# A spectral transformer block: another queue for an early load, full-height line products, new planner ranks, and another order in two feed-forward items

## The chip, the cores and the metric

The kernel runs on one NeuronCore of a Trainium2 chip. Five engines work side by side, each with its own queue that is worked off in order: TensorE (PE, matrix products, with weight loads listed as PEld), VectorE (DVE), ScalarE (ACT), GpSimd (POOL) and SyncE (SP, which here only starts transfers). SP, ACT and POOL can all start DMA transfers. The engines wait for each other by semaphores. The metric is the device time of one execution in microseconds (us); the profile gives one such execution, with every instruction's start and length.

## What is computed

The input is x with 2048 rows of 512 values (S = 2048, D = 512), the inner width of the feed-forward is F = 1792. Everything is 32-bit floating point. Cut to what matters, the reference is:

```python
mod = (silu(c) @ w_mod).reshape(1, 6, 1, -1)
sa, ca, ga, sb, cb, gb = (mod[:, n] for n in range(6))

h = layernorm(x) * (1 + ca) + sa
a = einsum("bsd,ed->bse", h, dft_hid_re)
b = einsum("bsd,ed->bse", h, dft_hid_im)
y = einsum("ts,bse->bte", dft_seq_re, a) - einsum("ts,bse->bte", dft_seq_im, b)
x = x + ga * y

h = layernorm(x) * (1 + cb) + sb
gate, up = h @ w1, h @ w3
x = x + gb * ((silu(gate) * up) @ w2)
```

So there is a Fourier mixing step along both axes (a product with the 512x512 and then with the 2048x2048 DFT matrices, of which only the real part is kept), and then a gated feed-forward, each behind a layer norm that is scaled and shifted by six vectors computed from c.

## The kernel before

**Precision.** Each 32-bit operand is split into a rounded high part (made by ACT) and the remaining low part (made by DVE or POOL as a subtraction). A product is then three passes on PE: high by high, low by high, high by low (`PASSES`). So each operand costs an ACT and a DVE or POOL instruction before PE can use it.

**Symmetry.** The kernel uses the symmetries of the DFT matrices: rows and mirrored rows of x are summed and subtracted, and a part of the sequence DFT is handled apart as "lines". Because it relies on these symmetries it checks the given matrices while it runs (instructions at line 1708, the tiles cx, cy, cz, cv). `judge` (lines 1759 to 1795) turns the outcome into one flag, by a chain of some twenty small DVE instructions. A branch at the end, taken only if the flag is set, holds a general version.

**The planned stage.** The first part, up to the first eleven products of the feed-forward, is a list of about 900 steps (`task`), each with a rank, the steps that it needs, and the engines that can do it, with a cost for each. Many can be done by DVE or POOL. `arrange` (lines 187 to 276) turns the list into an order when the program is built. It looks at all steps whose needs are met, takes those that could begin within 0.3 us of the soonest, and among them the one with the lowest rank, then the earliest end. The sum of a base rank, `KIND_BY[kind]` and `STEP_BY[name]` is the rank. The planner's own clock starts from times written by hand (`at(...)`, `clear.update(...)`). [...] To the end of a POOL candidate it adds `LOCK`. The order that comes out is fixed: on the chip each engine does its instructions in that order and waits where it must. Where the plan shows PE idle in the first part, the program puts filler products in (`keep_warm`, line 599).

Ahead of the planned steps stand some written in a fixed order (lines 447 to 459 and 2204 to 2229): the first loads, twelve filler products of 128x512, the statistics, root and scaling of row block 0, its transposes on PE (`turn_rows`, line 827), and the vectors sa and ca (scaled rows of w_mod summed by `mod_add`, line 626, and by PE, `mod_sum`, line 637). `load_x(1)` starts on SP only the loads of one side of row block 1. Those of the other side are started by ACT (`load_side(1, nc.scalar)`, line 2211), behind the statistics of block 0 and ahead of its square root (`norm_root`, line 792). The hidden DFT's blocks (`load_hid`, line 394) follow on SP. They are read by `shift_product` (line 729) and scaled by `w_highs` and `w_lows`.

The hidden DFT of block k is `hid_product` (line 929) and `hid_difference` (line 948). The sequence DFT comes in eight pieces (b, o): `seq_piece` (line 1295) and then `seq_lines` (line 1325), which adds the lines. In `seq_lines` the products with `sel` have 64 rows (the contraction runs over 64 partitions), their neighbours 128. `sel` holds one nonzero per column, made by `count_columns` and `spread_lines`. It multiplies `yc`, the first 64 partitions of a tile `gm_tile`, whose other half holds nothing.

Behind the sequence DFT stands the second layer norm for row blocks b = 0 and 1: `all_gates` and `add_rows` (DVE, line 1431), squares and root on ACT, scaling, transposes (`turn_block`, line 1474), the modulated tiles `xc`, their split (`h2h`, `h2l`), the sums of `xc` (tasks `tt`) and the split of these (`th`, `tl`). The copies `xm` (`keep_sums`) save x for the output. The tasks `jw1` and `jw3` split the first weights w1 and w3, with their sums `w1s` and `w3s` (`weight_jobs`).

**The feed-forward.** It has 14 items (g, pair): for each pair of row blocks, seven slices g of 256 of the 1792 inner columns. For gate (`a`) and up (`b`) an item has seven products instead of eight, a scheme with sums of operands: `a1` to `a7` and `b1` to `b7`, each two times three passes of 512 columns, 1.36 us of PE. `TO` names the bank into which a product accumulates: 1, 6, 7 and 4 into one, 2 into a second, 5 and 3 into a third. A result of the second row block is the first bank behind 1, 6 and 7 plus product 5. Before the change, 5 is copied out by ACT and added by DVE to the bank when 7 is there:

```python
dst = vs[i][q][:, k, :] if w == "w1" else own
plus(dst, to, own)          # DVE reads the bank `to`
result(i, w, q, k, dst)
```

The `b` results are multiplied with the gate's and split into `hf`, by `behind(1, ...)` on ACT and `behind(2, ...)` on DVE, one and two units later in the program. A `y` is one product with w2 (`down_unit`, six passes), and for the last two slices of the second pair DVE adds its result to x (line 1890) and the output is stored.

The order of an item is written out as a string. Units with a minus belong to the item before:

```python
head = "-b7 a1 a2 -b4 -b3 "
body = "a6 a5 y y a7 y a3 y a4 y b1 y b2 y b6 b5 y"
```

Item 7 (`turning`) is the first of the second pair of row blocks; its operands `th` and `tl` are made while the five `y` at its start run. In item 13, the last, `J` marks where the remaining checks and `judge` are put into the queues.

## Time and profile before

| | us |
|---|---|
| median of 3 runs | 640.85 (639.34 to 643.79) |
| the profiled execution, device time | 641.07 |
| its span, first to last instruction | 639.3 |
| mean granted clock of TensorE | 0.982 |

The span is cut in the profile's views by engine, by source line and by stretch of time. A row of the timeline holds the start, the length, the engine, the line and operation, the tile written and the tiles read, the shape, the count of merged instructions, and in brackets the engine's idle time before it with what ended it. "ACTq" and "SPq" rows are DMA issues on these queues. A row of the busy time by stretches holds the stretch, its length, the busy time of PE, PEld, DVE, ACT and POOL with the number of instructions, then the granted clock, the mean busy share of the DMA engines and GB/s. A row of the chain holds a start, a length and what the chain ran through. Matmuls overlap, and their ends are modelled, so the distance between two starts says more than a length.

### The profile page before, as it was taken

The numbers are of one execution on the slowest core, as the hardware profiler recorded it, in microseconds if no ns is written. First come the engines' busy times: TensorE is split into PE (matmuls) and PEld (weight loads), VectorE is DVE, ScalarE is ACT, GpSimd is POOL, SyncE is SP. The second block draws the span as 40 slices with busy tenths as digits, with TensorE's granted clock in tenths as the row PEclk, the third lists the DMA queues.
The fourth block names the chain that finished last, engine by engine and source line by source line (L and its number), as shares of the span: only waits on it lengthen the run. The fifth ranks groups of instructions, "written<-read, shape, count | busy, mean of one in ns | idle before, by whom it ended". The sixth has DMA issues, their size and how long they took to land.

```text
span 639.3 us, 8734 instructions
## 1 busy us (share of the span) xinstructions
PE 607.3 (95%) x2893; PEld 491.5 (77%) x2893; DVE 514.1 (80%) x1017; ACT 391.0 (61%) x626; POOL 215.2 (34%) x234
## 2 busy tenths in 40 slices
PE   8998899999969999989999999899999999999984
PEld 3778889767747888868877888687878888888864
DVE  4997879889986998468947797699888979879883
ACT  2587787527665557976875666485656556665310
POOL 7344114483951022103023321510553344434000
PEclk9999999999969999999999999899999999999998
DMA  7762345798143398738679967999999999999406
GB/s 243 220 192 71 100 110 155 224 249 226 66 157 107 91 204 207 131 103 172 137 151 262 269 173 149 239 190 195 261 285 258 260 229 261 238 253 269 145 1 136
DMA packets 61585, 118.11 MB, mean 185 GB/s; under 512 B 10649, under 2 KB 29081, under 8 KB 61532
## 3 DMA queue, kind: packets, MB, share of 16 engines
q1 hardware_dynamic: 45068, 67.66, 38.3%
q0 software_dynamic: 13536, 46.93, 33.3%
q10 hardware_dynamic: 2928, 2.88, 1.6%
q8 instruction: 24, 0.39, 0.3%
q14 instruction: 29, 0.24, 0.1%
HBM read 84.94 MB, written 35.65 MB: 189 GB/s over the span
## 4 chain that ended last, share of the span: by engine, by line
PE 71%; DVE 11%; issue 8%; DMA 5%; ACT 3%; POOL 1%; DVEq 0%; ACTq 0%; POOLq 0%
PE banks L106 53%; PE banks L1295 4%; DMA sum<-y 3%; PE banks L929 3%; PE banks L1325 2%; DVE w3s L100 2%; PE banks L1474 2%; PE banks L599 1%; DMA wmr<-in_wmr 1%; PE banks L948 1%; PE banks L827 1%; PE banks L729 1%; DVE w1s L100 1%; DVE x L94 1%; DVE ml L100 1%
## 5 line engine op out<-in xcount | busy, mean ns | idle before, releaser
L106 PE MATMUL banks<-hf,w2h 128*128 128x512 f32 (+1 forms) x452 | 141.5, 393 | 6.2 <-DVE hf L91 3.1
L1899 POOL DMA_DIRECT2D sum<-y x48 | 44.7, 931 | 244.5 <-ACT y L656 206.4
L106 PEld LDWEIGHTS banks<-hf,w2h 128*128 128x128 f32 x452 | 84.9, 189 | 26.4 <-DVE hf L91 5.0
L106 PE MATMUL banks<-hf,w2l 128*128 128x512 f32 (+1 forms) x226 | 88.1, 390 | 0.0
L656 ACT ACTIVATE y<-banks,gb 128x512 f32<-128x512 f32 x96 | 65.5, 683 | 27.3 <-PE banks L106 24.0
L88 ACT ACTIVATE hf<-v 128x512 fp32r<-128x512 f32 x56 | 35.3, 631 | 62.4 <-DVE v L97 53.5
L94 DVE TENSOR_TENSOR x<-banks,x 128x512 f32<-128x512 f32 x42 | 28.9, 689 | 43.2 <-PE banks L106 40.4
L88 ACT ACTIVATE x<-banks 128x512 f32<-128x512 f32 x84 | 48.8, 591 | 18.2 <-PE banks L106 16.5
L1983 ACT ACTIVATE v<-v 128x512 f32<-128x512 f32 x42 | 26.5, 632 | 39.7 <-DVE v L94 38.9
L106 PEld LDWEIGHTS banks<-hf,w2l 128*128 128x128 f32 x226 | 42.9, 190 | 8.7
L94 DVE TENSOR_TENSOR v<-banks,x 128x512 f32<-128x512 f32 x42 | 28.9, 688 | 19.4 <-PE banks L106 19.0
L91 DVE TENSOR_TENSOR hf<-v,hf 128x512 fp32r<-128x512 f32 x56 | 38.4, 686 | 4.0 <-ACT hf L88 3.7
L106 PE MATMUL banks<-th,w3sh 128*128 128x512 f32 x84 | 33.2, 395 | 0.3 <-ACT x L88 0.3
L106 PE MATMUL banks<-th,w1sh 128*128 128x512 f32 x84 | 32.9, 392 | 0.0
L106 PE MATMUL banks<-tl,w1sh 128*128 128x512 f32 x84 | 32.8, 390 | 0.0
L106 PE MATMUL banks<-th,w3sl 128*128 128x512 f32 x84 | 32.7, 390 | 0.0
L106 PE MATMUL banks<-th,w1sl 128*128 128x512 f32 x84 | 32.7, 390 | 0.0
L106 PE MATMUL banks<-tl,w3sh 128*128 128x512 f32 x84 | 32.7, 389 | 0.0
L599 PE MATMUL banks<-tmp 128*128 128x128 f32 (+1 forms) x140 | 27.9, 350 | 3.1 <-DVE tmp L489 3.1
L97 DVE TENSOR_TENSOR v<-v,x 128x512 f32<-128x512 f32 x42 | 29.2, 695 | 1.4
L599 PEld LDWEIGHTS banks<-tmp 128*128 128x128 f32 x140 | 19.6, 199 | 11.5 <-issue 8.4
L1295 PE MATMUL banks<-us,mh 128*128 128x512 f32 x64 | 25.9, 404 | 0.0
(361 smaller groups left out, 1694.3 us busy)
## 6 DMA issues: line engine op xcount, KB each, us to landing
sum<-y POOLq DMA_DIRECT2D x48, 512.0 KB
w<-in_w SPq DMA_DIRECT2D x42, 512.0 KB
wmc<-in_wmc SPq DMA_DIRECT2D x8, 512.0 KB
cx<-in_ctr SPq DMA_DIRECT2D x16, 256.0 KB
cz<-in_ctr SPq DMA_DIRECT2D x16, 256.0 KB
cx<-in_cti SPq DMA_DIRECT2D x16, 256.0 KB
cz<-in_cti SPq DMA_DIRECT2D x16, 256.0 KB
sum<-xm SPq DMA_DIRECT2D x8, 512.0 KB
```

The lines of the kernel that those rows point to most:

```text
L88: nc.scalar.activation(dst, src, AF.Copy, scale=scale)
L91: nc.vector.tensor_tensor(out=dst, in0=a, in1=b, op=OP.subtract)
L94: nc.vector.tensor_tensor(out=dst, in0=a, in1=b, op=OP.add)
L97: nc.vector.tensor_tensor(out=dst, in0=a, in1=b, op=OP.mult)
L100: (nc.gpsimd if engine == "POOL" else nc.vector).tensor_tensor(out=dst, in0=a, in1=b, op=op)
L106: nc.tensor.matmul(acc, lhs[a], rhs[b], start=first and n == 0, stop=last and n == len(PASSES) - 1, skip_group_check=more,)
L599: nc.tensor.matmul(warm[:, :width], onesf[:, :P], onesf[:, :width], start=True, stop=True)
L656: nc.scalar.activation(dst, src, AF.Identity, scale=by)
L929: nc.tensor.matmul(halves(hb[k])[:, m, :], sides((hh, hl)[a][k])[:, dt, m, :], wu[dt][:, b, m, :], start=False, stop=dt % 2 == 1 and n == ...
L1295: nc.tensor.matmul(acc(b, m), (mh, ml)[p][b, o][:, m, cols(a)], (us, ul)[q][k][:, m, :], start=(o, a, n) == (0, 0, 0), stop=False, skip_gr ...
L1899: nc.gpsimd.dma_start(sums[t, d // 2], y, accum_op=OP.add)
L1983: behind(k != 0 or q == 0, lambda: nc.scalar.activation(v, src, AF.Silu))
```

## The change

It has five parts.

1. `load_side` goes away. `load_x(1)` starts the loads of both sides of row block 1 on SP, ahead of the hidden DFT's blocks; ACT's two loads ahead of `norm_root(0)` are gone. The initial fillers are seven instead of twelve.
2. The products with `sel` in `seq_lines` take all 128 partitions. For this the other half of `gm_tile` is set to zero once (`clear_z`, DVE), and `count_columns` and `spread_lines` write all partitions.
3. `LOCK` is 50 instead of 0.6.
4. All of `KIND_BY` and `STEP_BY` is replaced (the new values run from about -950 to 620), and some of the hand-written times and costs of the planner change with it. So the order of the whole planned stage is a new one.
5. In items 6 and 13 (`split_blocks`) product 7 comes ahead of 5: the bank behind 1, 6 and 7 is copied out by ACT, and product 5's bank is added to the copy by DVE. Then 4, which ends the first row block, comes ahead of 5 and 3. The down products of such an item are queued behind `b4` instead of behind `b3`. The strings of items 6 and 13 and the head of item 7 change.

```diff
-    LOCK = 0.6
+    LOCK = 50.0
...
-        if par and other:
-            load_side(k, other)
-        elif par:
-            pass
+        if par:
+            load_own(xz[k][:, 1, :], lambda i: x[i], NK - 1 - i, 1, other)
         else:
             load_mirrored(xz[k][:, 1, :], x_rows, i, 0)
...
         if dt % 2 == 0:
-            load_x(1 + dt // 2, nc.sync if dt else None)
+            load_x(1 + dt // 2)
...
             set_to(zz[:, n, :], 0.0)
+        set_to(gm_tile[64:, 0, :], 0.0)
...
-        ints = sel["t"][:64, 0, :].bitcast(I32)
+        ints = sel["t"][:, 0, :].bitcast(I32)
...
-            sel["eo"[n % 2]][:64, n // 2, :], sel["t"][:64, 1, :],
-            signs[:64, TAU : TAU + 1], signs[:64, share : share + 1],
+            sel["eo"[n % 2]][:, n // 2, :], sel["t"][:, 1, :], col(TAU), col(share),
...
-            terms.append((acc(b, m), sel[x][:64, m, cols(b)], yc[0][:64]))
+            terms.append((acc(b, m), sel[x][:, m, cols(b)], yc[0]))
...
+        kept, added = (7, 5) if split_blocks(i) else (5, 7)
...
-        if n == 5:
+        if n == kept:
             st["y"] = take(F32, "x")
-        if n in (1, 5, 6):
-            copy(st["y" if n == 5 else "x"][:, n // 6, :], to)
+            copy(st["y"][:, 0, :], to)
+        elif n in (1, 6):
+            copy(st["x"][:, n // 6, :], to)
...
     KIND_BY = {
-        "add": -88, "all": 16, "cmp": 89, "diff": -17, "ect": 58, "eq": 55, "gate": 52,
...
+        "add": -501, "all": 88, "check": 169, "cmp": 395, "cx.d": 57, "diff": -147, "ec":
...
+        "gk": 104, "gtc": -517, "gtt": -361, "hh": -557, "hl": 97, "inverse": -185, "jw":
+        -281, "keep": -253, "lsq": 199, "m": 397, "m.d": 52, "mh": 129, "mine": -82, "ml":
...
-    keep_warm(12)
+    keep_warm(7)
...
-    load_side(1, nc.scalar)
     norm_root(0)
...
-    at(10.0, "turn0.0", "turn0.1")
-    at(16.2, "modp")
+    at(12.6, "turn0.0", "turn0.1")
+    at(15.8, "modp")
...
-            task(f"qm{m}.{dt}", r + dt, ["modr", f"w{dt}", *before], lambda m=m, dt=dt: shift_product(m, dt), PE=0.93)
+            task(f"qm{m}.{dt}", r + dt, ["modr", f"w{dt}", *before], lambda m=m, dt=dt: shift_product(m, dt), PE=0.5)
...
+    def split_blocks(i):
+        return i in (turning - 1, len(items) - 1)
...
+        if i == turning - 1:
+            body = "a6 a7 y y a4 y a5 y a3 y b1 y b2 y b6 b7 y"
         if i == len(items) - 1:
-            body = "a6 y a5 y b1 a7 y a3 b2 a4 y b6 b5 y b7 J y b4 b3 " + "y " * 10
-        head = "-b7 a1 a2 -b4 -b3 "
+            body = "a6 y b1 a7 y b2 a4 y b6 y b7 y b4 y J a5 y a3 y b5 y b3 " + "y " * 7
+        head = "-b4 a1 a2 -b5 -b3 " if i == turning else "-b7 a1 a2 -b4 -b3 "
```

More of the change, by code (lines that the diff above doesn't have):

```diff
@@ L368, in load_x @@
         load_own(xz[k][:, 0, :], lambda i: x[i], i, par)
-        if par and other:
-            load_side(k, other)
-        elif par:
-            pass
+        if par:
+            load_own(xz[k][:, 1, :], lambda i: x[i], NK - 1 - i, 1, other)
         else:
             load_mirrored(xz[k][:, 1, :], x_rows, i, 0)
-    def load_side(k, queue):
-        load_own(xz[k][:, 1, :], lambda i: x[i], NK - 1 - where(k)[0], 1, queue)
     wm = {}
@@ L1226, in count_columns @@
         sel["t"] = take(F32, "st")
-        ints = sel["t"][:64, 0, :].bitcast(I32)
+        ints = sel["t"][:, 0, :].bitcast(I32)
         nc.gpsimd.iota(ints, [[1, N]], base=0, channel_multiplier=0)
-        nc.gpsimd.tensor_copy(sel["t"][:64, 1, :], ints)
+        nc.gpsimd.tensor_copy(sel["t"][:, 1, :], ints)
     def spread_lines(n):
@@ L2129, in factor @@
         else:
-            own = st["y" if n == 7 else "x"][:, n % 2 if n < 7 else 0, :]
-            q, k = {2: (0, 0), 3: (0, 1), 7: (1, 1)}[n]
+            own = st["y"][:, 0, :] if n == added else st["x"][:, n % 2, :]
+            q, k = {2: (0, 0), 3: (0, 1), added: (1, 1)}[n]
             dst = vs[i][q][:, k, :] if w == "w1" else own
@@ L2135, in factor @@
             result(i, w, q, k, dst)
-            if n == 7:
+            if n == added:
                 behind(1, lambda: give(st["y"]))
@@ L2150, in folded @@
     KIND_BY = {
-        "add": -88, "all": 16, "cmp": 89, "diff": -17, "ect": 58, "eq": 55, "gate": 52,
-        "gtc": -105, "hl": 7, "line": -11, "lines.q": 39, "modf.d": 54, "odd": 21, "odd.r":
[3 rows of a table removed]
+        "add": -501, "all": 88, "check": 169, "cmp": 395, "cx.d": 57, "diff": -147, "ec":
+        -116, "ect": -315, "ectt": -68, "en": -188, "eq": 222, "ex": -600, "fw.d": 219,
+        "gk": 104, "gtc": -517, "gtt": -361, "hh": -557, "hl": 97, "inverse": -185, "jw":
+        -281, "keep": -253, "lsq": 199, "m": 397, "m.d": 52, "mh": 129, "mine": -82, "ml":
+        -573, "modv": -93, "odd": -178, "odd.r": -950, "og": 428, "prod": -62, "prod.q":
+        116, "qh": -368, "ql": -200, "qr": -514, "root": -510, "rowr": 197, "rsum": -274,
+        "rw": 140, "s": 620, "selt": 200, "st": -329, "stage.q": 50, "stats": 92, "sum":
+        -41, "tables": 313, "tl": 515, "turn": -151, "ul": -45, "ulh": 125, "up": -500,
+        "us": -194, "ush": -401, "wd": -269, "wdd": -123, "x.q": 85,
     }
     STEP_BY = {
[17 rows of a table removed]
[14 rows of a table added]
     }
@@ L2229, in folded @@
     hid_begin(0)
-    at(10.0, "turn0.0", "turn0.1")
-    at(16.2, "modp")
+    at(12.6, "turn0.0", "turn0.1")
+    at(15.8, "modp")
     task("modr", -99, ["modp"], lambda: (mod_read(1), mod_read(0)), DVE=0.5)
     for dt in range(ND):
-        at((17.2, 19.0, 24.3, 26.6)[dt], f"w{dt}")
+        at((17.0, 19.3, 24.0, 27.0)[dt], f"w{dt}")
     raw = [f"w{dt}" for dt in range(ND)]
@@ L2246, in folded @@
     for k in range(1, 4):
-        at((15.0, 21.1, 28.9)[k - 1], f"x{k}")
+        at((15.4, 21.4, 29.5)[k - 1], f"x{k}")
     at(18.3, "signs")
-    clear.update(PE=16.2, DVE=15.2, ACT=14.0, POOL=18.3, SP=26.6)
+    clear.update(PE=15.8, DVE=15.0, ACT=13.8, POOL=18.3, SP=26.8)
     def load_task(name, rank, needs, fn, slots, us, sp=0.6, pool=0.0):
@@ L2493, in folded @@
             f"c{u}", r + (2 if n > 1 else 14), [f"s{u}.1", *before_c, "yc", "es3", "sel3", "rowr5", "rw1"],
-            lambda b=b, o=o: seq_lines(b, o), PE=1.62 + 0.25 * o + 3.3 * ((b, o) == (0, 1)),
+            lambda b=b, o=o: seq_lines(b, o), PE=1.0 + 0.25 * o + 3.1 * ((b, o) == (0, 1)),
         )
@@ L2710, in unit @@
             down_banks[:] = [6, 7, 0, 1, 2]
-        if (kind, n) == ("a", 7 if i == turning else 3) and more:
+        if (kind, n) == ("a", 7 if i == turning else 5 if split_blocks(i) else 3) and more:
             load_w(("w3", *items[i + 1]))
@@ L2724, in unit @@
                 weight_jobs(i + 1, "w3")
+        if (kind, n) == ("b", 4 if split_blocks(i) else 3):
             if (g, pair) in SEVEN:
@@ L2731, in unit @@
             weight_jobs(i + 1, "w3")
-        beside(1.36, FACTOR[kind][n])
+        beside(1.36, FACTOR[kind][12 - n if split_blocks(i) and n in (5, 7) else n])
     operand = {1: "h2l{0}.0", 2: "h2l{0}.1", 3: "h2l{1}.1", 5: "tl1", 6: "tl2", 7: "tl3", 4: "tl4"}
```

34 rows, old and new, of tables (KIND_BY, STEP_BY) are left out of this document.

## The prediction

> **What bounds the kernel now.** I read the page first, then the busy time by stretches of 16 us, then the chain that ended last, and last each engine's timeline in the places that these point to.
>
> ```profile
> span 639.3 us, 8734 instructions
> PE 607.3 (95%) x2893; PEld 491.5 (77%) x2893; DVE 514.1 (80%) x1017; ACT 391.0 (61%) x626; POOL 215.2 (34%) x234
> ```
> ```profile
> 144.00:160.00 16.00, 16.00 (x74) 12.01 (x73) 14.78 (x32) 12.20 (x26) 5.75 (x4) 1.00 0.81 223
> 160.00:176.00 16.00, 15.74 (x87) 12.47 (x85) 14.47 (x8) 9.78 (x12) 15.26 (x6) 1.00 0.16 66
> 176.00:192.00 16.00, 9.82 (x25) 6.80 (x26) 13.47 (x15) 10.20 (x11) 8.40 (x4) 0.59 0.45 160
> ...
> 400.00:416.00 16.00, 13.63 (x52) 10.51 (x51) 10.96 (x14) 8.11 (x13) 8.76 (x8) 0.89 0.99 238
> ```
>
> TensorE (PE) is busy for 607.3 of 639.3 us, so only time in which it waits, idles on fillers, or runs at a lower clock can be won. The columns of the second view are PE, weight loads, VectorE (DVE), ScalarE (ACT) and GpSimd (POOL), then the granted clock. Two stretches stand out: 176 to 192 (PE 9.82 of 16, clock 0.59) and 400 to 416 (13.63, clock 0.89). The rest of the feed-forward is PE without gaps. The start and the last 20 us are read below. The sum is made against this execution's own 641.07 us, 0.03% above the median of the three runs, 640.85.
>
> **The start.**
>
> ```profile
> 10.12 0.18 DVE L788 BATCH_NORM_AGGREGATE mv<-st 128x2 f32<-128x6 f32 x1
> 15.31 0.17 DVE L796 RECIPROCAL rs<-rs 128x2 f32<-128x2 f32 x1 [5.01 <-ACT rs L792]
> ```
> ```profile
> 12.54 2.39 ACTq L289 DMA_DIRECT2D x<-in_x  x2
> 14.98 0.30 ACT L792 ACTIVATE rs<-mv,eps 128x2 f32<-128x2 f32 x1 [7.00 <-DMA x<-in_x]
> ```
> ```profile
> 4.08 8.45 DMA wmr<-in_wmr
> ...
> 23.21 0.86 PE banks L729 x2
> ...
> 26.83 3.35 PE banks L599 x30
> ```
> ```profile
> 3.08 13.18 PE L599 MATMUL banks<-tmp 128*128 128x512 f32 x24 [3.08 <-DVE tmp L489]
> ```
> ```profile
> 16.68 2.51 SPq L289 DMA_DIRECT2D x<-in_x  x4
> ```
>
> The statistics of the first row block stand at 10.12 + 0.18 = 10.30. The root (L792) that needs them is in ACT's queue behind the two loads of the second block's other side. These start only at 12.54, when an array of w_mod has landed (4.08 + 8.45 = 12.53), and last 2.39, so the root runs at 14.98 and DVE idles 5.01. With the loads on SyncE (SP) the root can run at about 10.35: 4.6 us earlier, and the reciprocal, the additions (L626) and the column sums move with it. The array of 12.53 is read first by the fourth of the five additions, which comes behind the reciprocal, a scaling and three additions, so I take it to be there in time. The warm-up must move too: 24 records in 13.18 end at 16.26. Seven of the twelve products are 14 records, at that mean 7.7 us, ending at 10.8, before the transposes, which follow the root by a reciprocal and a scaling. Had the twelve stayed, PE would take back most of the gain.
>
> Against it stand two more loads on SP, ahead of the hidden DFT's blocks and all that SP loads later. Four such issues take 2.51 (16.68), so two put the queue back by 1.26. The first product that reads such a block (L729) is at 23.21 and would move to 18.6. No row shows when the block lands, so I bound the gain: 4.6 if it is hidden, 4.6 - 1.26 = 3.3 if the queue's delay comes through once, and 2 if it does so again at a later block. I take **4.2**, near the upper end, since PE does not wait for data here at present: the 30 fillers at 26.83 (3.35 us on the chain) are put in by the planner, whose times are about as early as the new start.
>
> The third value that `clear_z` sets is one DVE instruction of half the height of the two that it has. It lies in DVE's wait for the first rows before 8.6 and costs nothing, or 0.4 if that wait goes. Counting and comparing on 128 partitions instead of 64 leaves the elements per partition as they are: nothing.
>
> **The line products.**
>
> ```profile
> 147.53 0.39 PE L1295 MATMUL banks<-us,ml 128*128 128x512 f32 x1
> 147.76 0.39 PE L1325 MATMUL banks<-ya,er 128*128 128x512 f32 x1
> 148.07 0.50 PE L1325 MATMUL banks<-ya,sel 64*128 64x512 f32 x1
> 148.50 0.49 PE L1325 MATMUL banks<-ya,er 128*128 128x512 f32 x1
> 148.93 0.50 PE L1325 MATMUL banks<-ya,sel 64*128 64x512 f32 x1
> 149.36 0.50 PE L1295 MATMUL banks<-us,mh 128*128 128x512 f32 x1
> ```
>
> Start to start, a product that follows one of its own shape takes 0.23 (147.53 to 147.76). With the 64-row ones between, four products take 149.36 - 147.76 = 1.60 instead of 0.92, and the next is late by 0.1. At full height each of the eight groups is 0.78 shorter: 6.2 us at most. In the row of 144 to 160 PE has no gap, so the time counts there, but the end of the stage hangs on the second layer norm, which waits only for the first four groups: 4 x 0.78 = **3.1**. The later groups only bring PE sooner to the wait below, unless that goes.
>
> **GpSimd and the new order.**
>
> ```profile
> 160.46 8.18 POOL L100 TENSOR_TENSOR h2l<-xc,h2h 128x1024 fp32r<-128x1024 f32 x3 [7.73 <-ACT h2h L88]
> 168.60 10.11 POOL L100 TENSOR_TENSOR xc<-xc,xc 128x1024 f32<-128x1024 f32 x4
> ```
> ```profile
> 176.44 2.55 DVE L100 TENSOR_TENSOR w1s<-w 128x256 f32<-128x256 f32 x1
> 179.03 0.43 DVE L100 TENSOR_TENSOR w1s<-w1s,w 128x256 f32<-128x256 f32 x1
> ```
> ```profile
> 169.40 1.03 ACT L88 ACTIVATE xm<-banks 128x1024 f32<-128x1024 f32 x1 [0.30 <-PE banks L1474]
> 180.16 1.06 ACT L88 ACTIVATE w1sh<-w1s 128x1024 fp32r<-128x1024 f32 x1 [9.73 <-DVE w1s L100]
> 181.12 1.01 ACT L88 ACTIVATE xm<-banks 128x1024 f32<-128x1024 f32 x1
> ```
> ```profile
> 182.18 0.69 PE L1474 MATMUL banks<-ident,xa 128*128 128x128 f32 x2 [6.43 <-ACT xm L88]
> ```
> ```profile
> 135.88 0.46 SPq L1804 DMA_DIRECT2D w<-in_w  x1
> ```
>
> While POOL subtracts (18.3 us in seven instructions), DVE's weight sums take 2.55 instead of 0.43, one POOL instruction each. ACT waits 9.73 for them, the copy that PE needs stands behind that in ACT's queue, and PE idles 6.43. Then it works at half clock: a mean of 0.59 is 13 of 16 us at half, so all of PE's 9.82 us there, which lose 4.9. So this place is worth up to 6.4 + 4.9 = 11.3.
>
> `LOCK` itself should change nothing. It is added to the end of a POOL candidate, but the planner compares rank before end, and only among candidates that begin within 0.3 us of the soonest. For one step on two engines, DVE's 1.22 plus 0.3 is below POOL's 2.4 plus 0.6 already; and where DVE is busy for longer, POOL is alone and is taken at any `LOCK`. What can help is the ranks. The weight steps ("jw") had base ranks of 101 to 107 beside the 103 of the sums of `xc`; they now get -281, the sums nothing. The load for `w1` (L1804) is issued at 135.88, 40 us before the row of 176.44. So they should be done before POOL's run. ACT could then copy at 170.4 and PE would not stop here. Next late is POOL's own run: its sums end at 178.7, and the third product of the feed-forward needs a rounding and a subtraction of them. Nothing excludes that other DVE steps are caught by POOL instead, with a wait like this one: the bounds are 11.3 won and 11.3 lost. I take half of the gain, **5.6**, since the row that makes ACT wait goes and the POOL rows stay.
>
> **The two items.**
>
> ```profile
> 407.18 0.50 PE L106 MATMUL banks<-hf,w2h 128*128 128x512 f32 x1 [2.34 <-DVE hf L91]
> ```
> ```profile
> 408.77 2.48 DVE L100 TENSOR_TENSOR xc<-xc,xc 128x1024 f32<-128x1024 f32 x2
> 413.95 1.22 DVE L100 TENSOR_TENSOR tl<-xc,th 128x1024 fp32r<-128x1024 f32 x1 [2.70 <-ACT th L88]
> ```
>
> ```profile
> 613.15 0.54 DVE cnt L1762 x4
> 616.98 0.66 DVE xr L1890
> ```
> ```profile
> 619.55 0.50 PE L106 MATMUL banks<-hf,w2h 128*128 128x512 f32 x1 [1.39 <-ACT hf L88]
> 620.82 0.50 PE L106 MATMUL banks<-hf,w2h 128*128 128x512 f32 x1 [0.77 <-DVE hf L91]
> ```
>
> Item 6: now `b4` stands before `a1 a2`, so the first down products find their operand. The wait of 2.34 goes, and the half clock behind it: 0.11 of 16 us lost, 1.8; 4.1 together. Next late are the operands of `a6` (`tl`): the sums that they need end at 411.25, so they end at 412.5 instead of 415.2. And `b5 -b3` now accumulate in one bank back to back: `b3` waits for DVE's read of it, 0.66 by the row of 616.98 and about 0.8 with both hand-overs, and that delays the sums too. So 1.9 is won, and 4.1 - 1.9 = 2.2 comes back as a wait ahead of `a6`. The row above shows a wait of 2.34 followed by half clock; half of that loss, 0.8, I take off: **1.1**, bounds 4 won and 1 lost. [...]
>
> Item 13: the verdict on the inputs (`J`) keeps DVE from 613.15 to 616.98, 3.8 us, and behind it PE waits 1.39 and 0.77, 2.2 together. In the new order the verdict stands before `a5`; behind it on DVE come `b4`'s low part and then `a5`'s sum, and `a3` writes the bank that the sum reads. PE covers `a5` and one down product: twelve steps of 0.23, 2.7. DVE needs the verdict and, before and behind it, three instructions of 0.66: 5.8. So PE waits 3.1 where the old 2.2 go, and with half of the clock loss again, 0.9, **1.8 is lost**. The bounds are 2.2 won, if DVE is ahead, and 5 lost, if checks of the inputs are still to be done there.
>
> Sum: 641.07 - 4.2 - 3.1 - 5.6 - 1.1 + 1.8 = 628.9.
>
> **The rivals.** One: PE stays the bound up to the feed-forward. Then seven groups count (5.5) and the whole 11.3: 641.07 - 4.2 - 5.5 - 11.3 - 1.1 + 1.8 = 620.8. For it speaks the row of 144 to 160 without a gap; against it POOL's rows. Two: the POOL part of the change does nothing, as argued of `LOCK`, and the new order keeps a wait like that of 182.18: 641.07 - 4.2 - 3.1 - 1.1 + 1.8 = 634.5. Three, on the other side: the new order lays POOL's run over the chain of the second layer norm, whose sums on DVE read two arrays as the held rows do. Each held step costs 2.55 - 0.43 = 2.1. From the 634.5 it takes more than three held steps to be slower than before; with eight it is 651. Five such steps per block stand there; against it: only one run of seven shows in these rows.
>
> **How the numbers follow.** Forecast 0.46, rival one 0.20, two 0.22, three 0.12. About 1% is what a measurement can tell from no change, so the bounds are 634.4 and 647.3. Faster: the forecast but for 0.01, rival one, and 0.05 of rival two: 0.70. Slower: 0.08 of rival three. Within 1%: 0.22. The range of 619 to 641 takes in the bounds of the start and the lines, rival two, and most of rival one; below it 0.08 is left and above it 0.12. The forecast's own range is 624 to 634.
>
> **What would show it.** The root (L792) at about 10.4 with no load ahead of it in ACT's queue, and the first L729 at 18 to 20. Steps of 0.23 in L1325 with 128 rows. No row of `w1s` or `w3s` at 2.5, and no PE wait of 6 us before the feed-forward. At the turn, PE waiting for `tl` in place of `hf`; at the end, one wait of 3 to 4 us on DVE before `a3`. It is wrong if SP's loads become a wait in the first 40 us, if DVE rows of 2.5 appear in the layer norm, or if a stretch of clock near 0.6 shows elsewhere.

## The result and the profile after

The changed kernel takes 651.62 us (median of 4 runs, 650.66 to 652.68), the kernel before 640.70 in the same comparison (4 runs, 639.34 to 643.79). The ratio is 1.0166 with a 95% interval of 1.0141 to 1.0190: the change costs 10.9 us. The profiled execution of the changed kernel took 652.03 us, its span is 650.2. Two executions in later comparisons, at a clock of 0.558, took over 1000 us (1007.49 of the kernel before, 1001.9 of one with the verdict late) and count in no ratio. In the changed kernel the source lines named here are lower by 5: L724 answers to L729, L787 to L792, L1290 to L1295, L1320 to L1325, L1469 to L1474, L1703 to L1708, L1885 to L1890.

Where the time went can be read from the first and the last start of the same products. The view of one tile's instructions gives them: duration min/median/max, then first to last start. `h2h,w1h` begins with the first product of the feed-forward and ends early in item 13, the last; `hf,w2l` ends with the last down product. The kernel before, tile w1h:

```profile
L106 PE MATMUL banks<-h2h,w1h x56: 389/389/794, 187.1 to 586.2; 128*128 128x512 f32 x56
```
and tile w2l:

```profile
L106 PE MATMUL banks<-hf,w2l x226: 279/389/632, 215.6 to 630.9; 128*128 128x512 f32 x111, 128*128 128x256 f32 x2
```

The changed kernel, tile w1h:

```profile
L106 PE MATMUL banks<-h2h,w1h x56: 389/389/776, 186.3 to 589.0; 128*128 128x512 f32 x56
```

and tile w2l:

```profile
L106 PE MATMUL banks<-hf,w2l x226: 279/389/628, 216.1 to 642.0; 128*128 128x512 f32 x111, 128*128 128x256 f32 x2
```

The feed-forward begins at 186.3 in place of 187.1: of the 12.9 us forecast for the first part, 0.8 arrived. Item 13 is reached 2.8 us later (589.0 and 586.2), and the last product starts 11.1 us later (642.0 and 630.9), so item 13 alone takes 8.3 us more. The first of these starts differs from one execution to the next: three of the kernels below, with the same planned stage instruction for instruction, reach the feed-forward at 180.4, 181.2 and 183.3. The last section comes back to this. The busy time by stretches of the changed kernel (PE, weight loads, DVE, ACT, POOL, then granted clock, DMA share, GB/s) shows where PE idles or runs slowly:

```profile
48.00:64.00 16.00, 12.67 (x82) 12.19 (x81) 12.03 (x22) 9.22 (x18) 8.30 (x7) 0.79 0.41 121
176.00:192.00 16.00, 6.74 (x25) 5.22 (x23) 12.55 (x18) 8.10 (x10) 10.08 (x4) 0.68 0.31 109
400.00:416.00 16.00, 15.20 (x66) 11.84 (x64) 10.20 (x13) 7.08 (x11) 7.17 (x6) 1.00 0.78 189
608.00:624.00 16.00, 9.34 (x35) 6.79 (x33) 10.89 (x42) 1.57 (x3) 0.00 (x0) 0.86 0.00 1
624.00:640.00 16.00, 15.52 (x57) 12.62 (x58) 9.17 (x14) 1.90 (x3) 0.00 (x0) 0.82 0.24 66
```

The stretch of 176 to 192 is worse than before (PE 6.74, was 9.82), 400 to 416 is better (15.20 at full clock, was 13.63 at 0.89), and there are two new bad places: 48 to 64 at a clock of 0.79, and the end, with PE busy for 9.34 of 16 us and a clock of 0.86 and 0.82.

**The start and the line products** did what was forecast. These are rows of the changed kernel's timeline (start, length, engine, line and operation), at the start:

```profile
9.77 0.29 ACT L787 ACTIVATE rs<-mv,eps 128x2 f32<-128x2 f32 x1 [1.78 <-DVE mv L783]
...
18.12 1.02 PE L724 MATMUL banks<-w,mod 128*97 128x512 f32 x2
```
and on PE near the end of the sequence DFT:

```profile
174.00 0.40 PE L1320 MATMUL banks<-ya,sel 128*128 128x512 f32 x1
174.24 0.40 PE L1320 MATMUL banks<-ya,er 128*128 128x512 f32 x1
```

The root runs at 9.77 (was 14.98) and the first L724 at 18.12 (23.05 in this view of the kernel before, 23.21 on its chain). The products with `sel` have 128 rows and start 0.23 to 0.24 apart from their neighbours, where the steps were 0.43. Counting takes 0.56 on 128 partitions (0.55 on 64), and the first comparison 0.55 (0.54); the three that follow run beside POOL's instructions of 112.94 to 118.65 and take 3.94 together.

**The stop ahead of the feed-forward** is still there. In the kernel before, the eight weight sums begin with those of w3 (DVE's timeline):

```profile
166.33 2.60 DVE L100 TENSOR_TENSOR w3s<-w 128x256 f32<-128x256 f32 x1
```

The timeline of DVE, POOL and ACT in the changed kernel:

```profile
162.01 8.42 POOL L100 TENSOR_TENSOR h2l<-xc,h2h 128x1024 fp32r<-128x1024 f32 x3
...
163.75 1.89 DVE L100 TENSOR_TENSOR w1s<-w 128x256 f32<-128x256 f32 x1
...
168.10 2.62 DVE L100 TENSOR_TENSOR w1s<-w 128x256 f32<-128x256 f32 x1
...
173.17 3.40 DVE L100 TENSOR_TENSOR w1l<-w,w1h 128x1024 fp32r<-128x1024 f32 x1
...
176.50 0.41 DVE L100 TENSOR_TENSOR w3s<-w 128x256 f32<-128x256 f32 x1
...
180.65 2.35 POOL L100 TENSOR_TENSOR w3sl<-w3s,w3sh 128x1024 fp32r<-128x1024 f32 x1 [5.16 <-DVE w1sl L100]
...
181.74 1.32 DVE L1703 SCALAR_TENSOR_TENSOR cy<-cy,cl 128x32 f32<-128x32 f32 x1
...
183.15 0.60 ACT L88 ACTIVATE ev<-banks 128x512 f32<-128x512 f32 x1 [3.08 <-issue]
```

and that of PE:

```profile
184.72 0.69 PE L1469 MATMUL banks<-ident,xa 128*128 128x128 f32 x2 [8.32 <-ACT xm L88]
...
192.31 0.50 PE L106 MATMUL banks<-tl,w1sh 128*128 128x512 f32 x1 [1.25 <-POOL tl L100]
```

The sums of w1 did move, from 176.44 to 163.75. But those of w3 now stand behind them, at 176.50 (were at 166.33), so the first of the eight comes only 2.6 us sooner. POOL's run of subtractions starts at 162.01, and beside it the four sums of w1 take 1.9 to 2.6 each (0.42 alone), and the subtraction `w1l` 3.40. ACT then waits 3.08 us, till 183.15. In the program as built, the copy `ev` that stands there takes over the buffer of `cy` and waits for DVE's last check of `cy`. That check (181.74) takes 1.32, until POOL's subtraction of `w3sl` ends (180.65 + 2.35 = 183.00); a check of the same shape takes 0.21 at 613.51. The copy that PE needs follows at 183.65, and PE stops for 8.32 us instead of 6.43. Later there is a new wait of 1.25 for a subtraction on POOL (192.31).

**The turn from item 6 to 7** (PE's timeline in the changed kernel). The old wait of 2.34 for `hf` is gone; these took its place:

```profile
377.67 0.50 PE L106 MATMUL banks<-th,w1sh 128*128 128x512 f32 x1 [1.78 <-ACT x L88]
...
398.26 0.50 PE L106 MATMUL banks<-th,w3sh 128*128 128x512 f32 x1 [0.69 <-ACT x L88]
...
407.50 0.50 PE L106 MATMUL banks<-h2h,w3sh 128*128 128x512 f32 x1 [0.78 <-DVE x L94]
...
417.66 0.50 PE L106 MATMUL banks<-tl,w1sh 128*128 128x512 f32 x1 [0.80 <-DVE tl L100]
```

The first three are hand-overs of a bank (`a6` to `a7`, `b6` to `b7`, `b5` to `b3`), the last is the operand `tl`. At 439.77 PE waits 1.59 more, for the sums that need item 8's w3.

**The last item** (timeline of DVE and PE in the changed kernel):

```profile
612.40 1.18 DVE L1703 SCALAR_TENSOR_TENSOR cv<-cz,cv 128x992 f32<-128x992 f32 x1
...
615.60 0.62 DVE L1757 TENSOR_SCALAR cnt<-cnt,mask 128x8 f32<-128x8 f32 x4
...
619.37 0.14 DVE L1790 TENSOR_SCALAR bad<-fine 1x1 int32<-1x1 f32 x1
...
620.04 0.67 DVE L94 TENSOR_TENSOR v<-banks,x 128x512 f32<-128x512 f32 x1
...
620.77 0.79 PE L106 MATMUL banks<-h2h,w1sh 128*128 128x512 f32 x1 [6.36 <-DVE v L94]
```

From 612.40 to 615.60 DVE does checks (L1703), to 619.44 the verdict, and then two steps for the products. PE, which has run out of products at 614.4, waits 6.36 us for the second of them, and its products then last 0.63 to 0.79 instead of 0.39: half clock (the granted clock is 0.50 from 620 to 628).

### The profile page after: what moved, and what is told of

Same layout as the page of the kernel before. It is cut to its first block, busy times and chain, and to the rows that moved or that the text cites. A ratio compares the mean times of both kernels' runs of the same rounds, so it can differ in the third digit from the quotient of the medians.

```text
span 650.2 us, 8760 instructions
## 1 busy us (share of the span) xinstructions
PE 604.0 (93%) x2905; PEld 495.1 (76%) x2905; DVE 518.8 (80%) x1017; ACT 387.8 (60%) x622; POOL 224.9 (35%) x239
## 3 DMA queue, kind: packets, MB, share of 16 engines
q10 hardware_dynamic: 2768, 2.62, 1.4%
## 4 chain that ended last, share of the span: by engine, by line
PE 68%; DVE 15%; DMA 6%; ACT 4%; issue 3%; SPq 2%; POOL 2%; DVEq 0%; ACTq 0%; POOLq 0%
PE banks L106 57%; PE banks L924 2%; PE banks L1290 2%; DMA w<-in_w 1%; SPq L389 1%; PE banks L943 1%; DMA wmr<-in_wmr 1%; DVE w1s L100 1%; PE banks L1181 1%; DMA w<-in_wdi 1%; PE banks L1469 1%; DVE x L94 1%; PE banks L822 1%; PE banks L594 1%; POOL tl L100 1%
## 5 line engine op out<-in xcount | busy, mean ns | idle before, releaser
L594 PEld LDWEIGHTS banks<-tmp 128*128 128x128 f32 x152 | 22.0, 210 | 9.7 <-issue 6.6
L1290 PE MATMUL banks<-us,mh 128*128 128x512 f32 x64 | 25.5, 399 | 0.3 <-ACT od L88 0.3
```

What stands on the lines that cost most here:

```text
L594: nc.tensor.matmul(warm[:, :width], onesf[:, :P], onesf[:, :width], start=True, stop=True)
L1290: nc.tensor.matmul(acc(b, m), (mh, ml)[p][b, o][:, m, cols(a)], (us, ul)[q][k][:, m, :], start=(o, a, n) == (0, 0, 0), stop=False, skip_gr ...
```

## The experiments

The theory after reading both traces: (1) the place of the verdict makes the loss in the last item; (2) the gains of the load and of the full height are real, and the new order of the planned stage takes them back; (3) GpSimd's run beside DVE makes the stop ahead of the feed-forward in both kernels; (4) in item 6 the waits only changed their places. The rivals are named in each expectation. Ratios are to the kernel before, each from runs beside it on the same chip. `LOCK` needed no run: with 0.6 and with 50 the planner makes the same order, instruction for instruction on every engine, with the old ranks and with the new.

**The last item.** The kernel after, with the old order of item 13:

```diff
     def split_blocks(i):
-        return i in (turning - 1, len(items) - 1)
+        return i in (turning - 1,)
...
-            body = "a6 y b1 a7 y b2 a4 y b6 y b7 y b4 y J a5 y a3 y b5 y b3 " + "y " * 7
+            body = "a6 y a5 y b1 a7 y a3 b2 a4 y b6 b5 y b7 J y b4 b3 " + "y " * 10
```

> The kernel after, but with item 13, the last, in its old order. Theory A (the verdict on the inputs, ahead of product a5, costs the most): in the trace of the changed kernel PE waits 6.36 us at 620.77, while DVE does checks and verdict from 612.40 to 619.44, and then works at half clock; the stretch from 600 us to the last matmul took 8.4 us more than before. So about 643 us, with waits of 1.4 and 0.8 near the end and none of 6. Theory B (the planned stage or item 6 carries most of the loss, and the wait at the end only takes the place of other waits): above 648 us.

Measured: 642.57 us, ratio 1.0048 (1.0019 to 1.0077) against 1.0166 with the new order: 1.2%, or 7.6 us, is item 13. The waits near the end are 1.35 and 0.76. Theory A holds.

The kernel after with only `J` moved:

```diff
-            body = "a6 y b1 a7 y b2 a4 y b6 y b7 y b4 y J a5 y a3 y b5 y b3 " + "y " * 7
+            body = "a6 y b1 a7 y b2 a4 y b6 y b7 y b4 y a5 y a3 y b5 y b3 y y J " + "y " * 5
```

> The kernel after, with the rest of the checks and the verdict (J) not ahead of product a5 of the last item but behind its last product b3 and two down products; all else as in the kernel after. Theory A (the place of the verdict alone makes the wait of 6.36 us and the half clock behind it): that wait goes, at most some 2 us come back as waits in the last five down products, and the time is 642 to 645. Theory B (the order of the products themselves, with a5, a3, b5, b3 so late, is at fault): 648 us or more, with PE waiting for sums on DVE among them.

Measured: 644.35 us, 1.0061 (1.0035 to 1.0086). Of the 7.6 us, 6.7 come back with the verdict's place; the waits left in the item are 0.90, 0.43 and 0.96. The traces agree on item 13: from the last start of `h2h,w1h` to that of `hf,w2l` it takes 53.0 in the changed kernel, 46.3 with its old order, 44.8 with the verdict late and 44.7 in the kernel before. So the products' new order does little harm, but nothing shows a gain by it either: the old order is as fast within the intervals.

**The load and the height.** Each of these is the kernel before with the hunks of that part of the change alone; the order of everything else stays the same.

The load:

```diff
-            load_x(1 + dt // 2, nc.sync if dt else None)
+            load_x(1 + dt // 2)
...
-    keep_warm(12)
+    keep_warm(7)
...
-    load_side(1, nc.scalar)
```

> The kernel before, with only the two loads moved from ACT's queue to SP's and seven fillers at the start in place of twelve; the order of all else as before. Theory A (as predicted): the start comes 4.2 us sooner and carries through, 636.5 us. Theory B (the gain is lost on the way, to transfers that come 1.3 us or more later on SP, or to steps that stand in the old order): the first L729 still moves from 23.2 to about 18.6, but the sequence DFT begins within 1 us of 90.4 and the time is 640 to 641.

Measured: 637.40 us, 0.9943 (0.9918 to 0.9968), 3.7 us won of 4.2 forecast. Theory A.

The height:

```diff
+        set_to(gm_tile[64:, 0, :], 0.0)
...
-            terms.append((acc(b, m), sel[x][:64, m, cols(b)], yc[0][:64]))
+            terms.append((acc(b, m), sel[x][:, m, cols(b)], yc[0]))
```

> The kernel before, with only the products with sel at 128 rows in place of 64; the order of all else as before. Theory A (as predicted): eight groups, each 0.78 us shorter, of which four count: 637.7 us, and steps of 0.23 in L1325. Theory B (PE only comes sooner to the wait of 6.43 at 182.18, which DVE's held weight sums set): the wait grows by what the groups save, and the time is 640 to 641.

Measured: 637.67 us, 0.9980 (0.9950 to 1.0011). Alone it is not settled: the medians are 3 us apart, the interval holds both theories. In its trace the stop ahead of the feed-forward has grown from 6.43 to 7.39, as theory B has it.

Both:

> The kernel before with the moved load, seven fillers and the full-height products, everything else in the old order. Theory A (the two gains are of different places, 3.6 and 1.3 us by the ratios measured alone, and add up): 635 to 636 us. Theory B (both end in the same wait of PE before the feed-forward, which the weight sums on DVE set): no better than the load alone, 637 us or more.

Measured: 633.28 us, 0.9895 (0.9855 to 0.9935). That is more than the sum of the two alone (0.9943 x 0.9980 = 0.9923), though within the intervals, and more than theory A gave. Together they are worth about 7 us, which is what the prediction has for these two terms (4.2 + 3.1).

**The new order of the planned stage.** The kernel after with all items in their old order. It differs from the one just shown in the ranks and in the planner's hand-written times and costs alone (`LOCK` changes nothing):

```diff
     KIND_BY = {
-        "add": -88, "all": 16, "cmp": 89, "diff": -17, "ect": 58, "eq": 55, "gate": 52,
+        "add": -501, "all": 88, "check": 169, "cmp": 395, "cx.d": 57, "diff": -147, "ec":
...
-    at(10.0, "turn0.0", "turn0.1")
+    at(12.6, "turn0.0", "turn0.1")
```

> The kernel after, but with all items of the feed-forward in their old order, so with the moved load, the full-height products and the new order of the planned stage. Theory A (the two items cost 8.4 and 2.3 us, the planned stage nothing either way): 641 us, with the wait of 8.3 us before the feed-forward as in the changed kernel. Theory B (the new order of the planned stage costs by itself): 645 us or more. Theory C (it brings what was predicted of it, 12.9 us): 628 us.

Measured: 641.04 us, 1.0014 (0.9978 to 1.0050). Theory A, and it says more: beside 0.9895 the new order costs 1.2%, 7.6 us, where 5.6 us gain were forecast. The starts show where: in the profiled executions the new order reaches the feed-forward 1.6 us later (181.2 and 179.6), its first `hf,w2l` 5.2 us later (211.0 and 205.8) and the last `h2h,w1h` 7.5 us later (585.0 and 577.5). So in these two executions most of the loss lies behind the first product of the feed-forward, and little of it ahead.

Is it GpSimd? In the kernel with load and height, the low parts and sums of `xc` and the weight sums may now only go to DVE:

```diff
-        task(f"h2l{t}.{i}", begun_f - 20 + n, [f"h2h{t}.{i}"], lows, 1, DVE=1.22, POOL=2.4)
+        task(f"h2l{t}.{i}", begun_f - 20 + n, [f"h2h{t}.{i}"], lows, 1, DVE=1.22)
...
-            ways = {"DVE": dve, "POOL": 2.05 * dve} if dve else {"ACT": act}
+            ways = {"DVE": dve} if dve else {"ACT": act}
```

and the tasks `tt` likewise.

> The same kernel as the one with the load and the height, but the low parts and the sums of xc and the weight sums at the end of the planned stage can be put on DVE only, so that GpSimd's run of seven subtractions there is gone. Theory A (POOL's run holds DVE's weight sums at 2.5 us in place of 0.43, and this sets the wait of 6.4 us and the half clock of 10 us behind it): the wait falls to 2 us or less, and the time by 6 to 11 us, to 625 to 630. Theory B (DVE has too much to do there in any case: seven steps of 1.22 more make 8.5 us, against eight holds of 2.1 that go): a wait of 5 us or more stays, and the time is within 2 us of the kernel with POOL's run.

Measured: 636.20 us, 0.9934 (0.9910 to 0.9959): not faster than with POOL's run, if anything slower, and neither theory holds as it was put: the stops that are left lie between A's 2 us and B's 5. Its timeline (DVE, POOL and PE):

```profile
167.86 5.79 POOL L100 TENSOR_TENSOR tl<-xc,th 128x1024 fp32r<-128x1024 f32 x2 [8.68 <-ACT th L88]
...
168.83 2.62 DVE L100 TENSOR_TENSOR w1s<-w 128x256 f32<-128x256 f32 x1
...
175.79 0.71 PE L106 MATMUL banks<-h2h,w1l 128*128 128x512 f32 x1 [4.75 <-DVE w1l L100]
...
181.71 0.80 PE L106 MATMUL banks<-h2h,w1h 128*128 128x512 f32 x1 [3.94 <-DVE ev L91]
```

PE reached the feed-forward 9.2 us sooner, at 170.40, but the planner had left two subtractions (`tl`) to POOL. They caught two of the sums `w1s` (2.62 and 2.44; the next takes 0.41), and PE stopped at the third product, for `w1l`, and again at a bank that DVE had yet to read. So I kept `tl` on DVE as well:

```diff
-        task(f"tl{n}", begun_f - 15 + m, [f"th{n}"], lambda e, n=n: lows(n, e), 1, DVE=1.22, POOL=2.4)
+        task(f"tl{n}", begun_f - 15 + m, [f"th{n}"], lambda e="DVE", n=n: lows(n, e), 1, DVE=1.22)
```

> The kernel without GpSimd's run of seven subtractions, with the low parts tl of the sums kept on DVE as well. There, PE reached the first product of the feed-forward at 170.40, 9.2 us sooner than with the run, but stopped at the third for 4.75 us (w1l: two of the sums w1s took 2.62 and 2.44 beside POOL's two subtractions of tl) and again for 3.94 us (the bank that DVE had still to read), with half clock behind. Theory A (each hold by POOL simply moves the stop to the next step that PE needs, and it goes once POOL is out of all of this place): w1s takes 0.42 each, the two stops are 4 us or less together, the half clock is 3.4 us or less, and the time is 5 to 8 us below the 633.3 of the kernel with load and height, 626 to 628. Theory B (DVE alone cannot do the work in time): stops of 6 us or more stay, and the time is 633 or more.

Measured: 632.91 us, 0.9883 (0.9846 to 0.9920), no gain to speak of over 0.9895. Its timeline (DVE and PE):

```profile
168.92 0.42 DVE L100 TENSOR_TENSOR w1s<-w 128x256 f32<-128x256 f32 x1
...
171.65 0.51 PE L106 MATMUL banks<-h2h,w1l 128*128 128x512 f32 x1 [0.55 <-DVE w1l L100]
...
179.11 0.68 DVE L91 TENSOR_TENSOR ev<-ev,banks 128x512 f32<-128x512 f32 x1
...
179.84 0.79 PE L106 MATMUL banks<-h2h,w1h 128*128 128x512 f32 x1 [6.98 <-DVE ev L91]
```

Now no sum is held (0.42), and the stop for `w1l` is down to 0.55. But PE then waits 6.98 for DVE's last read of a bank (179.11), which stands in DVE's queue behind `tl` and `w3l`. GpSimd held the sums, and with GpSimd gone the order on DVE makes a stop of nearly the same length: both theories have a part of it. The next run puts these reads first:

```diff
     STEP_BY = {
-        "all1.0": 38, "all2.0": 9, "all2.1": 29,
+        "all1.0": 38, "all2.0": -300, "all2.1": -300, "all3.0": -300, "all3.1": -300, "own2": -300, "own3": -300,
```

> The kernel with load and height, GpSimd out of the end of the planned stage altogether, and in addition the reads of the last row blocks' banks (the steps all2 and all3) with a rank that puts them ahead of the low parts and weight sums on DVE. Theory A (PE's stop of 6.98 us before the second product of the feed-forward is the wait for such a read, which DVE did at 179.11, behind 8 other steps): the stop falls by 3 us or more, the half clock behind it to 3.4 us or none, and the time to 628 to 630, against 632.9. Theory B (DVE has as much to do in any order, and PE waits for another of its steps instead): the stops there still make 6 us or more, and the time is 632 or more.

Measured: 629.76 us, 0.9835 (0.9771 to 0.9899), as theory A has it. PE's timeline in this kernel:

```profile
178.87 0.50 PE L106 MATMUL banks<-th,w1sh 128*128 128x512 f32 x1 [2.90 <-ACT x L88]
```

and its busy time in the stretch of 176 to 192:

```profile
176.00:192.00 16.00, 11.29 (x46) 8.40 (x47) 14.24 (x26) 9.23 (x14) 2.44 (x2) 1.00 0.43 158
```

The longest stop is 2.90, and the clock is 1.00 (0.59 in the kernel before). Two of the four reads still stand late; the intervals of this kernel and the one with load and height (0.9835 and 0.9895) overlap a little, so what this place alone is worth is shown by the traces and not settled by the times.

The same edit as in the first of these three, made to the new order:

> The planned stage of the kernel after (load, height, new ranks and times), the old items, and GpSimd without its subtractions and sums of xc and without weight sums at the end of the stage. Theory A (the new order loses its 7.7 us there, by POOL's subtractions beside DVE): the stop of 8.32 us before the feed-forward falls to 5 or less, and the time to 634 to 637. Theory B (it loses them elsewhere, or by what DVE has to do): 639 us or more, with stops of 8 us or more in the same place.

Measured: 636.81 us, 0.9943 (0.9911 to 0.9974) against 1.0014: 0.7%, 4.5 us, come back. PE's timeline:

```profile
176.67 0.44 PE L1469 MATMUL banks<-ident,xa 128*128 128x128 f32 x2 [1.11 <-ACT xm L88]
...
182.51 0.50 PE L106 MATMUL banks<-th,w1sh 128*128 128x512 f32 x1 [2.00 <-ACT x L88]
185.56 0.80 PE L106 MATMUL banks<-tl,w1sh 128*128 128x512 f32 x1 [2.56 <-POOL tl L100]
```

The stop of 8.32 is now three of 1.11, 2.00 and 2.56. So more than half of the new order's loss goes with GpSimd's run there. The traces say the same: from the first transposes of the second layer norm (L1469, 155.25 here and 150.62 in the kernel with the old items) to the feed-forward (177.51 and 181.25) it takes 22.3 us in place of 30.6. What the rest is stays open; one thing that adds to it in some executions is shown in the last section.

**Item 6.** The kernel before with item 6 alone changed, a `y` between `a6 a7` and between `b6 b7`, and `a1 a2` between `b5` and `b3`:

```diff
-            body = "a6 a7 y y a4 y a5 y a3 y b1 y b2 y b6 b7 y"
+            body = "a6 y a7 y a4 y a5 y a3 y b1 y b2 y b6 y b7"
...
-        head = "-b4 a1 a2 -b5 -b3 " if i == turning else "-b7 a1 a2 -b4 -b3 "
+        head = "-b4 -b5 a1 a2 -b3 " if i == turning else "-b7 a1 a2 -b4 -b3 "
```

> The kernel before with only item 6 changed, the other way about than in the kernel after: product 7 ahead of 5 as there, but a down product between a6 and a7 and between b6 and b7, and a1 a2 of item 7 between b5 and b3, so that no product follows at once on another one of the same bank. Theory A (in the kernel after, the waits of 1.78, 0.69 and 0.78 us at these three places are hand-overs of a bank, and they eat the gain of the wait of 2.34 and the half clock behind it): these waits fall below 0.3 each, the wait of 2.34 is gone, and the time is 3 to 4 us below before, 637. Theory B (the gain is given back later in item 7, at the operands tl or at the load of w3): 640 us or more, with a wait there.

Measured: 643.93 us, 1.0058 (1.0035 to 1.0081), slower than before. The three hand-overs are gone but for one of 0.69, now between `b7` and `b4`, which share a bank too. The loss comes later. SP's timeline in this kernel:

```profile
420.55 4.45 SPq L1853 DMA_DIRECT2D out<-sum  x6
425.10 0.75 SPq L1804 DMA_DIRECT2D w<-in_w  x1
```

and that of ACT and PE:

```profile
432.90 1.06 ACT L88 ACTIVATE w3h<-w 128x1024 fp32r<-128x1024 f32 x1 [4.23 <-DMA w<-in_w]
...
436.99 0.79 PE L106 MATMUL banks<-th,w3h 128*128 128x512 f32 x1 [3.56 <-DVE x L94]
```

The load of item 8's w3 is issued at 425.10, behind stores of finished rows that occupy SP from 420.55. In the kernel before it is issued at 424.89, also behind such stores, and ACT waits 0.39 for it; here ACT waits 4.23, and PE stops for 3.56. So the stores were put six units later:

```diff
-                behind(8, lambda i=d // 2: store(t, i))
+                behind(14, lambda i=d // 2: store(t, i))
```

> The kernel with only item 6 changed and its products kept apart, in which the stores of the first pair's finished rows are issued six units later, so that the load of w3 for item 8 stands ahead of them in SP's queue and not behind six of them. Without that, the load was issued at 425.10 and w3 was read at 432.90, and PE waited 3.56 us and fell to half clock for 6.8 us. Theory A (item 6's gain of 2 us is given back by that load, held up in SP's queue by stores that wait for GpSimd's accumulating transfers): the load is issued before 421, the wait is below 0.5 us, and the time is 5 to 6 us less than the 643.9 without it, 638. Theory B (the load is late because the DMA engines are full, 1.0 of their time there): the wait stays at 2 us or more, and the time above 642.

Measured: 641.78 us, 1.0016 (0.9998 to 1.0034). The load is issued by 414.9 and PE's waits at that place fall from 3.56 to 0.83 and 0.46, so the queue was the cause of the wait, as theory A has it. But the time is 3.8 us above the 638 that A gave, and not to be told from the kernel before. So in this form too, item 6's order gains nothing that can be measured; why not stays open.

**The verdict in the old order**, behind `b3` and three down products, in the kernel with load and height:

```diff
-            body = "a6 y a5 y b1 a7 y a3 b2 a4 y b6 b5 y b7 J y b4 b3 " + "y " * 10
+            body = "a6 y a5 y b1 a7 y a3 b2 a4 y b6 b5 y b7 y b4 b3 y y y J " + "y " * 7
```

> The kernel with the load and the height, in the old order of the last item, with the verdict behind b3 and three down products in place of ahead of b4. Theory A (the waits of 1.40 and 0.77 us near the end come from the verdict's 3.8 us on DVE): they go, DVE has 0.6 us to spare per down product afterwards and ends at most 1.5 us late; 631 to 632.5 us against 633.3. Theory B (in the last down products DVE is the bound): no change or up to 2 us slower, with DVE busy to the end.

Measured: 632.15 us, 0.9868 (0.9846 to 0.9890) beside 0.9895 (0.9855 to 0.9935): both waits are gone, but the intervals overlap, and DVE ends with a backlog of eight additions. Joined with the reads of the banks first (two down products here):

```diff
-b7 y b4 b3 y y y J " + "y " * 7
+b7 y b4 b3 y y J " + "y " * 8
```

> The kernel of e12 with the verdict behind b3 and two down products in the last item. Theory A (the two add up, each being worth what it is alone): 1 us below e12, the waits of 1.4 and 0.8 us near the end gone. Theory B (the verdict only moves DVE's backlog to the last additions and their stores): the same as e12 within 0.5 us.

Measured: 629.39 us, 0.9822 (0.9759 to 0.9884), not to be told from 629.76. By its median this is the fastest kernel of the study, 1.8% faster than before: load, full height, GpSimd out of the end of the planned stage, banks read first, verdict late, old items otherwise.

## Why the prediction was wrong, step by step

| term of the sum | forecast | measured | by |
|---|---|---|---|
| start (load) | -4.2 | -3.7 | the load alone |
| line products | -3.1 | -3.1 | load with height, less load |
| GpSimd and new order | -5.6 | +7.6 | old items, less load with height |
| items 6 and 7 | -1.1 | +2.2, not settled | old item 13, less old items |
| item 13 | +1.8 | +7.6 | after, less old item 13 |
| sum | -12.2 | +10.6 | |

The measured column is the difference of two ratios, times 640.7; the sum is that of 1.0166, by the medians it is 10.9.

The measured 651.62 lies 10.6 us above the upper end of the range. The new order (13.2 us from its forecast) and item 13 (5.8) make 19.0 of the 22.7 us of error.

**The start and the lines** were right in mechanism. The gain of the start carried through, as taken, near the upper end of its bounds. The size of the lines' gain is less sure than the table looks: measured alone it is 1.3 us and not told from nothing (0.9950 to 1.0011), and PE gives 1.0 us back in the stop ahead of the feed-forward, which grows from 6.43 to 7.39.

**GpSimd and the new order** was the step that failed most. That `LOCK` changes nothing was right. The step that failed is "So they should be done before POOL's run": it took the lower rank of the weight steps for an early start. The sums of w1 did come 12.7 us earlier, right into the run, which still holds each of them (1.9 to 2.6). The step showed only the one held sum of w1 at 176.44; four held sums of w3 stood before it, from 166.33, and the new order mainly let w1 and w3 change places. Rival two ("the new order keeps a wait like that of 182.18") is what happened there, with a longer wait (8.32). The rest was not foreseen: that ACT then waits 3.08 us ahead of that copy for the buffer of a check that POOL holds too (this was not tried by itself), and a second wait behind the first product of sums (1.25). And one thing was wrong in the frame: "this place is worth up to 6.4 + 4.9 = 11.3" supposed that nothing stands behind the held sums. With POOL away they took 0.42, and PE stopped all the same, for DVE's reads of the banks, until these were moved too; then 2.90 was left.

**Items 6 and 7.** The wait of 2.34 went and so did the half clock, as said; the hand-over from `b5` to `b3` is 0.78 (407.50), where 0.8 was forecast, and the wait for `tl` is 0.80 instead of 2.2. What the step missed is two more hand-overs of one bank in the same string: `a6 a7` (1.78, since ACT, which must copy the bank out, was rounding `w3h` and a part of `hf`) and `b6 b7` (0.69). And it stopped looking at `a6`: 1.59 more at 439.77 are w3 arriving late, a wait that the two runs on item 6 trace to the stores ahead of its load on SP's queue.

**Item 13** had the right mechanism, the verdict ahead of a step that PE needs, and the wrong size: "So PE waits 3.1" stood for 6.36. In the kernel before, the checks ended just ahead of the verdict (DVE's timeline):

```profile
612.34 0.67 DVE L1708 SCALAR_TENSOR_TENSOR cx<-cx 128x496 f32<-128x496 f32 x1
```

The step took them as done; in the new order DVE still had 3.2 us of them (612.40 to 615.60) ahead of the 3.8 us of the verdict. This case was named as a bound ("5 lost, if checks of the inputs are still to be done there") and not counted. The bound was too low as well: the half clock behind so long a wait (0.86 and 0.82 over two stretches) was put at 0.9 and is about 4.1. The products run at half clock from 620.77 to 629.77, 0.43 from start to start in place of 0.23; less a wait of 0.78 that is 8.2 us, of which half is lost.

**The rivals.** Three foresaw the sums of the second layer norm held by POOL, and its 651 for eight held steps lies close to the measured 651.62. That is luck: in the changed kernel the steps of L1426 take 0.69 each from 144.83 to 152.65, none is held, and item 13 alone makes 7.6 us of the time. What POOL held were the weight sums again, a subtraction and checks beside them, and steps near 50 us (below). None had item 13 as the thing that decides, and with 7.6 us it does, together with the new order.

## What to carry to other kernels

When a wait is taken away, list what PE needs next and in which queue position each of these stands; here the stop ahead of the feed-forward was the first of several of nearly the same length, and only moving more than one of them paid. Put long work that no one waits for (a verdict, checks, stores) behind the work that frees a buffer or a bank, and count all that is left of it where it is placed. Of an order by ranks, ask where each step lands in time beside the other engine's work, not only that it comes earlier.

## What the hardware showed that was not expected

In these traces the half clock does not follow from the length of a wait alone. The kernel before and the kernel with the banks read first both have a wait of 2.34 us at the turn of item 7. The first lost clock there (0.89 in 400 to 416, with 0.50 from 408 to 411), the second did not. PE's timeline of the second:

```profile
393.10 0.50 PE L106 MATMUL banks<-hf,w2h 128*128 128x512 f32 x1 [2.34 <-DVE hf L91]
```

and its busy time around it:

```profile
384.00:400.00 16.00, 13.62 (x59) 10.65 (x58) 12.02 (x15) 7.79 (x12) 9.58 (x9) 1.00 0.98 223
400.00:416.00 16.00, 16.00 (x72) 13.22 (x71) 14.59 (x20) 12.51 (x18) 1.70 (x3) 1.00 1.07 233
```

So the wait of 2.34 was followed by half clock in one execution and not in another, and the 1.8 us of lost clock that the prediction joins to this wait are not lost with every wait of that length. What else decides it, no run shows.

A copy of four columns took 3.12 us in one execution. Timeline of POOL and DVE, in the new order without POOL's run:

```profile
53.09 4.68 POOL L100 TENSOR_TENSOR hl<-hs,hh 128x1024 fp32r<-128x1024 f32 x2
...
54.68 3.12 DVE L844 COPY hs<-hs 128x4 f32<-128x4 f32 x1
```

and in the changed kernel:

```profile
50.33 3.98 DVE L802 TENSOR_SCALAR x<-x,rs 128x512 f32<-128x512 f32 x2
...
51.69 2.33 POOL L100 TENSOR_TENSOR hl<-hs,hh 128x1024 fp32r<-128x1024 f32 x1
...
57.26 0.17 DVE L844 COPY hs<-hs 128x4 f32<-128x4 f32 x1
```

The copy of 128x4 takes 3.12 beside POOL's subtractions and 0.17 alone; two scalings of x take 3.98 (1.00 in the kernel with the old items). PE waits 3.05 behind the copy (1.42 at that place in the kernel with the old items) and 2.30 behind the scalings, and in 48 to 64 the clock is 0.89 in the first kernel and 0.79 in the second. In the profiled executions of the kernels with the old items and with the old item 13, whose planned stage is that of the changed kernel instruction for instruction, there is nothing of it, and they reach the feed-forward 5 to 6 us sooner (181.2 and 180.4, against 186.3). So the same order is caught in one execution and not in another. How often was not measured; it may be a part of the loss that stayed open above. In these rows a copy (3.12) and scalings (3.98), which read one array, are long beside POOL's subtractions too; the prediction counted on held steps only among instructions that read two.
